# A mask table read by SyncE, zero products between TensorE's own, and loads behind flags in an attention and MLP kernel

## The chip, the cores and the metric

The kernel runs on one core of one Trainium2 chip. A time is the device time of one execution in microseconds (us). The time before is 322.92 us, the median of 9 executions (320.95 to 325.45). One more execution was recorded by the hardware profiler; its span, from the first to the last instruction, is 321.2 us and its own time 322.98 us. All shares and waits below come from that one.

## The reference

Two blocks follow each other. The first is block-sparse attention over 4 batches, 8 heads, 768 positions and 64 values per head:

```python
scores = scale * np.matmul(q, k.transpose(0, 1, 3, 2))
# mask: neighbouring blocks of 32, the first and last block, 3 sampled blocks for each block row
scores = np.where(mask, scores, -1000000000.0)
attn = softmax(scores)
x = np.matmul(attn, v)
```

The mask is the same for all batches and heads. The second block mixes tokens and channels, with `w_tok` 768x768, `w_ch1` 512x2048 and `w_ch2` 2048x512:

```python
u = x + lam * einsum('ts,bsd->btd', w_tok, alpha1 * x + beta1)
out = u + lam * (np.maximum((alpha2 * u + beta2) @ w_ch1, 0) @ w_ch2)
```

Inputs and the output are float32; the kernel computes its products in 16-bit types.

## The kernel before

**Units and pairs.** The 32 (batch, head) combinations are worked off as 16 pairs of heads, pair `p` being two heads of batch `p // 4`. Each pair has nine units (`NU`), and a unit is 128x1024 scores in one PSUM tile `sps`, of which there are two. TensorE makes the scores, ScalarE turns them into exponentials in an `eT` tile, TensorE multiplies these by V (with a column of ones, so that the row sums come out too) into the PSUM tile `ops`, and VectorE divides (L614, L617) into `x_sb`.

**Two ways of masking.** The first six pairs (`single`, L642, L657, L682) carry the mask in the scores product itself, as 24 more rows of the contraction. The other ten (`paired`, L720, L746, L751, L778) make the scores of two heads side by side in the two halves of the array and clamp the exponentials against a table `maskT`, 128 x 9 x 512 in f16: VectorE takes the minimum at L751. The table's 24 distinct rows are made by `mrow` (L470); `mout` (L476) writes them to DRAM, each 32 times, and `min_` (L479) reads the whole table back. Both transfers are issued by POOL.

**Heads.** Q and K reach SBUF by POOL's loads (L305, with a cast to bf16, in `ld` buffers), VectorE casts them into a `rel` buffer (L492; two buffers), and they are transposed into `qx` and `kx`: for the first six pairs by TensorE (L211) with copies out of PSUM by ScalarE (L269) or VectorE (L271), for the others by two DMA transposes that SyncE issues (L581). V is copied into a `vext` buffer (L800).

**The MLP.** When a pair is normalised, VectorE makes `a1p`, TensorE multiplies it by the transposed `w_tok` (L854), VectorE adds (L864) and makes `ub` (L870), which is transposed into `uT` by TensorE (batch 0) or by a DMA (L901). When a batch's `uT` is complete, its first layer (L927), the ReLU (L938 on ScalarE, L942 on VectorE) and the second layer (L972, in the PSUM tiles `cp` and, once attention is over, `ops`) can run. `w2b`, which holds the second layer's weights, is scaled by `lam` on VectorE (L455) after it has landed.

**The order.** While the kernel is built, a planner decides the order in which each engine's instructions are written. Every piece of work is a `Job` with an engine, an assumed duration, a priority and the buffers that it takes and gives back. The planner goes through time, and whenever an engine is free it takes the ready job of the best priority. The chip then runs each engine's instructions in that order. POOL's loads have a fixed order, and the planner has its own notion of when a load lands (`xfer`, `dma_free`). A `gate` holds scores back that run too far ahead of the MLP. PV of batch 0 may use `ops` or `cp` (the `take` at the PV job), since the MLP does not need `cp` yet. At the start, `keep_warm` issues products of a zero tile `warm` (L169), which shares its buffer with the `eT` tiles.

Of the kernel before, what the change touches and what calls it, by code (L numbers as in the profile page):

```python
# [12 lines left out]
F16 = mybir.dt.float16  # L13
BF = mybir.dt.bfloat16
# [6 lines left out]
S = 768  # L21
D = 64
BLK = 32
NBLK = S // BLK
# [3 lines left out]
P = 128  # L28
NT = S // P
# [6 lines left out]
NU = 9  # L36
NS = NPAIR * NU
NPE = 6
NET = 11
LEAD = 18  # L40
NLD = 7
AHEAD = 13000.0
SCALE = 1.0 / 8.0
EXPB = -0.35667494
# [21 lines left out]
def kernel(  # L66
# [19 lines left out]
    nc = tc.nc  # L86
# [22 lines left out]
    wk = ctx.enter_context(tc.tile_pool(name="work", bufs=1))  # L109
# [50 lines left out]
    for i in range(1, NQB):  # L160
        nc.sync.dma_start(kx[i][MB, :], ind_dr.ap())

    warm = wk.tile([P, 512], BF, name="warm", tag="eT", bufs=NET)
    nc.vector.memset(warm[:], 0.0)
    wps = ps.tile([P, 512], FP, name="cp", tag="cp", bufs=1)

    def keep_warm(n, w):
        for _ in range(n):
            nc.tensor.matmul(wps[:, 0:w], warm[:, 0:P], warm[:, 0:w], start=True, stop=True)  # L169

    keep_warm(9, 512)
    for t in vext:
# [21 lines left out]
            op1=ALU.mult,  # L194
        )

    rel0 = wk.tile([P, 2, NT, 2 * D], BF, name="rel", tag="rel", bufs=2)

    def first_cast(a):
        for i, src in enumerate((q2f, k2f)):  # L200
# [31 lines left out]
    for j in range(2, NQB):  # L232
# [11 lines left out]
    DRAIN = 166.0  # L244
    free_at = dict(NONE=0.0, PE=T0, ACT=T0, DVE=T0, POOL=4800.0, SP=T0)
    slots = dict(
        sps=2, mm=2, cp=1, ops=1, eT=NET, head=NQB, vext=NV, ld=NLD, rel=2,
        x=NXB, uT=3, hts=2, a1p=2, ub=2, ot=2, w2b=1,
    )
    jobs = []  # L250
# [2 lines left out]
    class Job:  # L253
        def __init__(self, eng, dur, prio, fn, deps=(), take=(), give=(), lat=None):
            self.eng = eng if isinstance(eng, tuple) else (eng,)
            self.dur, self.prio, self.fn = dur, prio, fn
            self.deps = list(deps)
            self.take, self.give = take, give
            self.lat = lat
            self.alt = {}  # L260
            self.xfer = None
            self.done = None
            self.gate = None
            self.n = len(jobs)
            jobs.append(self)
# [31 lines left out]
    def Load(xfer, prio, fn, deps=(), take=()):  # L297
        j = Job("POOL", 720.0, prio, fn, deps, take)
        j.xfer = xfer
        return j  # L300

    def load(name, src_ap, shape, dt, tag, bufs, xfer, prio, deps=(), take=()):
        def fn():
            t = wk.tile(shape, dt, name=name, tag=tag, bufs=bufs)
            nc.gpsimd.dma_start(t[:], src_ap)  # L305
            return t

        return Load(xfer, prio, fn, deps, take)
# [3 lines left out]
    w2tile = []  # L312
    wtk_tile = []

    def load_pair(p, prio, which="qkv"):
        for src, dt, nm in ((q, BF, "q2"), (k, BF, "k2"), (v, F16, "v2")):
            if p == 0 and nm != "v2" or nm[0] not in which:
                continue
            ld[p, nm] = load(
                nm, pair_ap(src, *pairs[p]), [P, 2, NT * D], dt, "ld", NLD,  # L320
                1300.0 if p < 2 else 980.0, prio, take=("ld",),
            )

    def plain(eng, dur, prio, fn, deps=(), **kw):
        return Job(eng, dur, prio, fn, deps, **kw)
# [57 lines left out]
        load_w1(g, next(order))  # L383
    load_pair(5, next(order))
    load_pair(6, next(order))
    mout_prio = next(order)
    w2_prio = [next(order) for _ in range(2)]
    min_prio = next(order)
    w2_prio += [next(order) for _ in range(2)]
    for p in range(7, len(pairs)):  # L390
        load_pair(p, next(order))

# [71 lines left out]


    rows = maskT[:].rearrange("p u c -> p (u c)")[:, 0:S]
    mask_dr = nc.dram_tensor("mask_rows", [NBLK, BLK, S], F16, kind="Internal").ap()

    def mrow():
        nc.vector.tensor_scalar(  # L470
# [2 lines left out]
        )  # L473

    def mout():
        nc.gpsimd.dma_start(mask_dr, rows[MB, :].unsqueeze(1).broadcast_to([NBLK, BLK, S]))  # L476

    def min_():
        nc.gpsimd.dma_start(  # L479
            maskT[:].rearrange("p u c -> p (u c)"),  # L480
            mask_dr.rearrange("g r c -> (g r) c").rearrange("(p o) c -> p (o c)", o=NT),
        )

    j = Job("DVE", 400.0, (3, 3, 9), mrow, [wtok_jobs[-1]])
    j = Load(5000.0, mout_prio, mout, [j])
    mask_jobs = [Load(5000.0, min_prio, min_, [j])]

# [9 lines left out]
        return ld[p, nm].out[:]  # L499

    head_ready = {}
    after = []

    def slot_of(p):
        return (2 * NPE + p - NPE) % NQB
# [2 lines left out]
    for p in range(len(pairs)):  # L508
# [25 lines left out]
        elif p < NPE:  # L534

            def rel_of(p, i):
                def f():
                    if i == 0:
                        rels[p] = wk.tile([P, 2, NT, 2 * D], BF, name="rel", tag="rel", bufs=2)
                    return rels[p][:, :, :, i * D : (i + 1) * D]  # L540

                return f

            cq = cast_job(p, 0, "q2", rel_of(p, 0), (2, p, 0), ("rel",))
            ck = cast_job(p, 1, "k2", rel_of(p, 1), (2, p, 1), (), [cq])
            prev = head_ready[2 * p - 1]
            for a in range(2):
                h = 2 * p + a

                def tr(p=p, a=a, h=h):  # L550
                    tl["hd", h] = transposes(rels[p], a)

                def cpq(eng, h=h):
                    copy(eng, qx[h % NQB][0:D, :], tl["hd", h][0:D, :])

                def cpk(eng, h=h):
                    copy(eng, kx[h % NQB][0:D, :], tl["hd", h][D:P, :])

                jt = Job("PE", mmt(NT, P), (2, p, a), tr, [ck, prev], take=("mm", "head"),
                         give=("rel",) if a else ())  # L560
                j1 = Copy((1, p, a), cpq, [jt])
                j2 = Copy((1, p, a), cpk, [jt])
                prev = head_ready[h] = Job("NONE", 0.0, (0,), lambda: None, [j1, j2], give=("mm",), lat=0.0)
        else:

            def stage_of(p, i):
                def f():
                    if i == 0:
                        rels[p] = wk.tile([P, 2, NT, P], BF, name="rel", tag="rel", bufs=2)
                    return rels[p][:, i, :, :].rearrange("p o (h d) -> p h o d", h=2)  # L570

                return f

            cq = cast_job(p, 0, "q2", stage_of(p, 0), (3, p, 0), ("rel",))
            if p > NPE + 1:
                after.append((cq, (p - 3) * NU))
            ck = cast_job(p, 1, "k2", stage_of(p, 1), (3, p, 1), (), [cq])

            def xt(p=p):
                for i, dst in enumerate((qx, kx)):  # L580
                    nc.sync.dma_start_transpose(  # L581
                        dst[slot_of(p)][:].rearrange("p (o c) -> p o c", o=NT),
                        rels[p][:, i, :, :].rearrange("p o c -> p (o c)"),
                    )

            prev = [head_ready[2 * NPE - 1]] if p == NPE else [head_ready[2 * p - 2]]
            jx = Job("SP", 2600.0, (1, p), xt, [ck] + prev, take=("head",), lat=2500.0,
                     give=("rel",))
            jx.slow = True
            head_ready[2 * p] = head_ready[2 * p + 1] = jx  # L590
# [36 lines left out]
    def single(p):  # L627
# [3 lines left out]
        for u in range(NU):  # L631
# [40 lines left out]
            for si, (s0, s1) in enumerate(segs):  # L672
# [20 lines left out]
                give = ("eT",) if s1 == hi else ()  # L693
                if s1 == 2 * HT:
                    give += ("vext",)
                take = ((("ops", "cp") if b == 0 else ("ops",), ("opsel", p, a)),) if first else ()
                prev_pv = Job("PE", mmt(s1 - s0, D + 1), (2, i, si), pv, deps, take=take, give=give)
                last_pv = prev_pv
                if s1 % HT == 0:
# [110 lines left out]
            single(p)  # L810
    for j, i in after:
        j.deps.append(qk_jobs[i])

# [237 lines left out]
    heapq.heapify(events)  # L1053
    seq = 100
    early = set()
    loads = sorted((j for j in jobs if j.xfer is not None), key=lambda j: (j.prio, j.n))
    t = 0.0
    left = len(jobs)
    pe_idle = []
    while left:  # L1060
        moved = True
        while moved:
            moved = False
            for e in free_at:
# [19 lines left out]
                for tk in j.take:  # L1084
# [6 lines left out]
                            st["ch2"] = True  # L1091
                    else:
                        slots[tk] -= 1
                j.out = j.fn(e) if len(j.eng) > 1 else j.fn()
                if getattr(j, "ch", False):
                    st["ch"] += j.dur
                if e == "PE" and t - free_at[e] > 1:
                    pe_idle.append((free_at[e], t))
                dur = j.alt.get(e, j.dur)
# [2 lines left out]
                free_at[e] = t + dur  # L1102
                lat = j.lat if j.lat is not None else DRAIN + SEM if e == "PE" else SEM
                j.done = t + dur + lat
                if j.xfer is not None:
                    dma_free[0] = max(dma_free[0], t + 2300.0) + j.xfer
                    j.done = dma_free[0] + 200.0
                    loads.pop(0)
                seq += 1
                heapq.heappush(events, (j.done, seq, j))  # L1110
                if e == "PE":
# [16 lines left out]
        while events and events[0][0] <= t:  # L1128
            _, _, j = heapq.heappop(events)
            if j is None:  # L1130
                continue
            for g in j.give:
                if isinstance(g, tuple):
                    slots[tl.pop(("slot", g))] += 1
                else:
                    slots[g] += 1
            for s in succ.get(j.n, ()):
                if (j.n, s.n) in early:
                    continue
                waiting[s.n] -= 1  # L1140
                if not waiting[s.n]:
                    for e in s.eng:
                        by_eng[e].append((t, s))
# [31 lines left out]
```

The softmax here doesn't subtract the row's maximum and nothing guards it: scores larger than these inputs give would overflow.

## Time and profile before

| | |
|---|---|
| median of 9 executions | 322.92 us |
| profiled execution, its own time | 322.98 us |
| its span | 321.2 us |
| granted TensorE clock over the span | 0.995 |
| TensorE (PE) busy | 307.0 us, 96%, 3238 products |
| ScalarE (ACT) busy | 208.0 us, 65% |
| VectorE (DVE) busy | 207.4 us, 65% |
| POOL busy | 44.3 us, 14% |
| DMA | 31.95 MB, mean 99 GB/s |
| mask write, issue to landing | 12.6 us |
| mask read, issue to landing | 9.0 us |

PE is TensorE's products and PEld its weight loads, which overlap them; POOL is GpSimd and SP is SyncE, which only issues transfers here. Products are pipelined and their ends are modelled, so a product's recorded duration is a latency: what counts is the pitch from one to the next. A line such as `X <- Y: 3.5, 8, 0.8` in the waits says that X's engine stood for Y's result for 3.5 us in total, 8 times, at most 0.8 us. A name such as L927 is a line of the kernel file.

### The profile page before, as it was taken

To read this page: it belongs to the slowest core of one execution; us is meant where nothing else is said; L and a number is where in the kernel's file an instruction comes from. 1 tells how busy PE (TensorE), PEld (TensorE's weight loads), DVE (VectorE), ACT (ScalarE), POOL (GpSimd) and SP (SyncE) were. 2 spreads that over 40 slices of the span, in tenths; PEclk is the share of its full clock that TensorE was granted. 3 is DMA by queue.
4 is the path that set the end of the run, shared out by engine and by line. 5 is a ranking of instruction groups with operands and counts; after the bars stand their busy time and mean duration, and the time that the engine had idled before them with its cause. 6 is when DMAs were issued, how large, how long until landed. Compare 5 with 4: busy or idle time off the path is not lost.

```text
span 321.2 us, 7610 instructions
## 1 busy us (share of the span) xinstructions
PE 307.0 (96%) x3238; PEld 189.1 (59%) x3238; DVE 207.4 (65%) x406; ACT 208.0 (65%) x264; POOL 44.3 (14%) x69
## 2 busy tenths in 40 slices
PE   7889989899699999999999999999999999999996
PEld 3566868667444556565655556565655575555544
DVE  4558977779578887877977688868677660201001
ACT  4979899897656667756686567755784526354530
POOL 4638142515001010100100000000000000000000
PEclk9979999999999999999999999999999999999999
DMA  6999999999999397724581231311100201201102
GB/s 147 182 246 203 210 236 173 265 191 124 138 130 208 63 123 80 101 59 111 56 111 46 57 61 24 59 25 69 23 4 35 76 16 24 100 0 53 48 23 75
DMA packets 46774, 31.95 MB, mean 99 GB/s; under 512 B 27516, under 2 KB 42264, under 8 KB 46612
## 3 DMA queue, kind: packets, MB, share of 16 engines
q0 software_dynamic: 16496, 17.83, 35.1%
q1 hardware_dynamic: 29992, 13.40, 22.1%
q8 instruction: 25, 0.41, 0.5%
q10 hardware_dynamic: 252, 0.24, 0.3%
q14 instruction: 9, 0.07, 0.1%
HBM read 32.04 MB, written 7.47 MB: 123 GB/s over the span
## 4 chain that ended last, share of the span: by engine, by line
PE 77%; DMA 13%; ACT 4%; DVE 2%; POOL 2%; issue 1%; DVEq 0%; ACTq 0%
PE mm L927 22%; PE cp L972 22%; PE mm L854 8%; PE ops L778 8%; PE sps L720 7%; DMA w2b<-in_moe_w_ch_dram 5%; DMA kx<-rel 4%; PE ops L972 4%; ACT eT L657 3%; DMA wtk<-in_moe_w_tok_dram 3%; PE sps L642 2%; PE sps L927 2%; PE ops L682 1%; DMA q2f<-in_q_dram 1%; DVE hts L942 1%
## 5 line engine op out<-in xcount | busy, mean ns | idle before, releaser
L746 ACT ACTIVATE eT<-sps 128x1024 f16<-128x1024 f32 x90 | 88.3, 1020 | 31.8 <-PE sps L720 30.5
L927 PE MATMUL mm<-uT,w1b 128*128 128x384 bf16 x472 | 90.6, 326 | 2.9 <-DVE x_sb L864 2.5
L938 ACT ACTIVATE hts<-mm,b1t 128x384 bf16<-128x384 f32 x91 | 52.9, 581 | 57.7 <-PE mm L927 55.0
L972 PE MATMUL cp<-w2b,hts 128*128 128x512 bf16 (+1 forms) x336 | 80.4, 374 | 0.3 <-DVE hts L942 0.3
L751 DVE TENSOR_TENSOR eT<-eT,maskT 128x1024 f16<-128x1024 f16 x90 | 61.0, 686 | 13.5 <-ACT eT L746 13.4
L927 PEld LDWEIGHTS <-w1b 128*128 128x128 bf16 x512 | 46.9, 97 | 37.0 <-issue 7.4
L972 PEld LDWEIGHTS <-hts 128*128 128x128 bf16 x400 | 36.5, 98 | 34.7 <-issue 1.4
L657 ACT ACTIVATE eT<-sps 128x1024 f16<-128x1024 f32 (+1 forms) x55 | 52.7, 1015 | 4.8 <-PE sps L642 4.3
L989 DVE TENSOR_TENSOR ot<-x_sb,cp 128x512 f32<-128x512 f32 (+1 forms) x21 | 14.1, 673 | 46.3 <-PE cp L972 45.7
L778 PEld LDWEIGHTS <-eT 128*128 128x128 f16 x720 | 29.7, 97 | 16.4 <-issue 3.6
L854 PE MATMUL mm<-a1p,wtokT 128*128 128x128 bf16 x576 | 36.6, 219 | 0.1
L642 PE MATMUL sps<-qx,kx 88*128 88x512 bf16 (+1 forms) x144 | 31.9, 330 | 4.4 <-ACT eT L657 3.5
L778 PE MATMUL ops<-vext,eT 128*128 128x65 f16 x720 | 35.5, 194 | 0.0
L854 PEld LDWEIGHTS <-wtokT 128*128 128x128 bf16 x576 | 33.0, 98 | 1.9 <-issue 0.5
L720 PE MATMUL sps<-qx,kx 64*128 64x512 bf16 (+1 forms) x240 | 27.3, 327 | 0.0
L942 DVE TENSOR_SCALAR hts<-mm,b1t 128x384 bf16<-128x384 f32 x27 | 16.5, 616 | 9.9 <-PE mm L927 9.7
L682 PEld LDWEIGHTS <-eT 128*128 128x128 f16 x432 | 19.4, 98 | 6.0 <-issue 0.8
L864 DVE TENSOR_TENSOR x_sb<-x_sb,mm 128x384 f32<-128x384 f32 x32 | 17.6, 551 | 7.3 <-PE mm L854 7.2
L642 PEld LDWEIGHTS <-kx 88*128 88x128 bf16 x144 | 12.8, 99 | 10.2 <-issue 5.6
L870 DVE TENSOR_TENSOR ub<-x_sb,a_bc 128x384 bf16<-128x384 f32 x32 | 17.2, 554 | 0.3
L720 PEld LDWEIGHTS <-kx 64*128 64x128 bf16 x240 | 8.1, 94 | 15.2 <-issue 12.5
L617 DVE TENSOR_TENSOR x_sb<-ops,rcp 128x384 f32<-128x384 f32 x28 | 15.6, 558 | 1.0
(74 smaller groups left out, 222.6 us busy)
## 6 DMA issues: line engine op xcount, KB each, us to landing
out_dram<-ot SPq DMA_DIRECT2D x23, 256.0 KB, 2.0
v<-in_v_dram POOLq DMA_DIRECT2D x16, 192.0 KB, 6.5
q<-in_q_dram POOLq DMA_DIRECT2D x15, 192.0 KB, 10.5
k<-in_k_dram POOLq DMA_DIRECT2D x15, 192.0 KB, 6.9
w1b<-in_moe_w_ch_dram POOLq DMA_DIRECT2D x4, 512.0 KB, 10.4
w2b<-in_moe_w_ch_dram POOLq DMA_DIRECT2D x4, 512.0 KB, 14.9
wtk<-in_moe_w_tok_dram POOLq DMA_DIRECT2D x3, 384.0 KB, 10.1
mask_rows<-maskT POOLq DMA_DIRECT2D x1, 1152.0 KB, 12.6
```

Of the source, the lines that this page charges most:

```text
L642: nc.tensor.matmul(sps[:, f - u * UN : f - u * UN + w], kx[h][0:KC, ts(jt, P)], qx[h][0:KC, c : c + w], start=True, stop=True,)
L657: nc.scalar.activation(eT[:, c], sps[:, c], AF.Exp, bias=EXPB, scale=SCALE)
L682: nc.tensor.matmul(ops[p, a][:, t * VW : t * VW + D + 1], eTs[p, u][:, ts(i - u * GU, P)], vx[:, a, jt, 0 : D + 1], start=(i % HT == 0), s ...
L720: nc.tensor.matmul(sps[:, a * 512 + lo : a * 512 + lo + w], kx[sl][r, ts(jt, P)], qx[sl][r, c : c + w], start=True, stop=True,)
L746: nc.scalar.activation(eT[:], sps[:], AF.Exp, bias=EXPB, scale=SCALE)
L751: nc.vector.tensor_tensor(out=e, in0=e, in1=maskT[:, u, :].unsqueeze(1).broadcast_to([P, 2, 512]), op=ALU.min,)
L778: nc.tensor.matmul(ops[p, a][:, t * VW : t * VW + D + 1], eTs[p, u][:, a * 512 + c * P : a * 512 + (c + 1) * P], vx[:, a, jt, 0 : D + 1], ...
L854: nc.tensor.matmul(tp[:, j, :], wtokT[:, s, ts(3 * g + j, P)], tl["a1p", p][:, s, :], start=(s == 0), stop=(s == NT - 1),)
L927: nc.tensor.matmul(hp[:, 0:HS], w1b[:, dk, ts(f, P)], uTs[b][:, dk, ts(hf, HS)], start=(dk == 0), stop=(dk == 3),)
L938: nc.scalar.activation(hts[kk][:, f, :], hp[:, 0:HS], AF.Relu, bias=b1t[:, f : f + 1], scale=1.0)
L942: nc.vector.tensor_scalar(out=hts[kk][:, f, :], in0=hp[:, 0:HS], scalar1=b1t[:, f : f + 1], scalar2=0.0, op0=ALU.add, op1=ALU.max,)
L972: nc.tensor.matmul(cps[kk, mi][:, 0:w], hts[kk][:, nk, ts(m, P)], w2tile[0][:, nk, lo : lo + w], start=(nk == 0), stop=(nk == 15),)
```

## The change

The change has five parts.

1. **The mask table.** Only the 24 rows are written to DRAM, once, by SyncE. SyncE reads the table with 18 transfers: transfer `c` fills the partitions `c`, `c + 16`, and so on, eight in all, and repeats one DRAM row over up to six of a partition's table rows; where the six straddle a block border, it is split in two. All this hangs in the planner's order on the scores of unit 28 (`MASK_AT`), no longer on the last of the `w_tok` copies. The four `w2b` loads come one after another in POOL's order. The planner knows the read as a job of SyncE that also delays loads in flight (`bulk`).
2. **Zero products.** `fill` writes products of the zero tile in front of a TensorE job wherever the planner sees TensorE idle for longer, as wide as the idle time allows (up to 512 columns), until the first second-layer job. They go to `cp`, so PV of batch 0 uses `ops` alone. The zero tile has a buffer of its own.
3. **Flags.** From pair 8 on, each load of q, k and v is preceded on POOL by a copy of one element of `flag` into `held_`, and VectorE sets that element (`raise_flag`). The planner ties the flag of pair `p` to the scores of unit `9 * (p - 2) + 2`, and 3 and 6 more for k and v; it used to tie the cast of q to unit `9 * (p - 3)`.
4. **Three stages.** `rel` has three buffers instead of two.
5. `ld` has six buffers instead of seven.

The line numbers shift: L642 becomes L676, L657 L691, L682 L716, L720 L754, L746 L780, L751 L785, L778 L812, L492 L529, L581 L615, L854 L889, L927 L962, L972 L1007.

```diff
-NLD = 7
+NLD = 6
+HOLD = 2
+MASK_AT = 28
...
-    warm = wk.tile([P, 512], BF, name="warm", tag="eT", bufs=NET)
+    warm = pp.tile([P, 512], BF, name="warm", tag="warm")
...
+    def fill(ns):
+        while ns > 60.0:
+            w = min(512, int(ns * 2.4))
+            keep_warm(1, w)
+            ns -= w / 2.4 + 3.0
...
-    rel0 = wk.tile([P, 2, NT, 2 * D], BF, name="rel", tag="rel", bufs=2)
+    rel0 = wk.tile([P, 2, NT, 2 * D], BF, name="rel", tag="rel", bufs=3)
...
+            if held is not None:
+                nc.gpsimd.tensor_copy(out=held_[0:1, held : held + 1], in_=flag[0:1, held : held + 1])
             t = wk.tile(shape, dt, name=name, tag=tag, bufs=bufs)
             nc.gpsimd.dma_start(t[:], src_ap)
...
+    def raise_flag(p, i):
+        c = 3 * p + i
+
+        def fn():
+            nc.vector.memset(flag[0:1, c : c + 1], 0.0)
+
+        j = Job("DVE", 70.0, (0, p), fn)
+        after.append((j, (p - 2) * NU + HOLD + 3 * i))
+        return [j]
...
-    mask_dr = nc.dram_tensor("mask_rows", [NBLK, BLK, S], F16, kind="Internal").ap()
+    mask_dr = nc.dram_tensor("mask_rows", [NBLK, S], F16, kind="Internal").ap()
...
     def mout():
-        nc.gpsimd.dma_start(mask_dr, rows[MB, :].unsqueeze(1).broadcast_to([NBLK, BLK, S]))
+        nc.sync.dma_start(mask_dr, rows[MB, :])
...
     def min_():
-        nc.gpsimd.dma_start(
-            maskT[:].rearrange("p u c -> p (u c)"),
-            mask_dr.rearrange("g r c -> (g r) c").rearrange("(p o) c -> p (o c)", o=NT),
-        )
...
+        dst = maskT[:].rearrange("p u c -> p (u c)").rearrange("p (o w) -> p o w", o=NT)
+        src = mask_dr.rearrange("(m f) w -> m f w", f=3)
+        for c in range(16):
+            o = 0
+            while o < NT:
+                f, r = divmod(NT * c + o, BLK)
+                e = min(NT, o + BLK - r)
+                nc.sync.dma_start(
+                    dst[c:P:16, o:e, :], src[:, f, :].unsqueeze(1).broadcast_to([8, e - o, S])
+                )
+                o = e
+
+    mrow_job = j = Job("DVE", 400.0, (2, 3, 9), mrow)
+    j = Job("SP", 400.0, (0, 0), mout, [j], lat=2500.0)
+    j = Job("SP", 7200.0, (0, 1), min_, [j])
+    j.bulk = 5500.0
+    mask_jobs = [j]
...
-                take = ((("ops", "cp") if b == 0 else ("ops",), ("opsel", p, a)),) if first else ()
+                take = ((("ops",), ("opsel", p, a)),) if first else ()
...
+                if e == "PE" and not st["ch2"]:
+                    fill(t - free_at[e] - 60.0)
```

## The prediction

> **What bounds the kernel now.** I read the slices of the page first, then a table of stretches, the waits of each engine, the timeline around the largest hole, and the chain in order of time for the pitch of each product.
>
> ```profile
> PE   7889989899699999999999999999999999999996
> ACT  4979899897656667756686567755784526354530
> PEclk9979999999999999999999999999999999999999
> ```
>
> TensorE leaves room only in the first third of the span, and there ScalarE is as full; one slice has a low clock. The stretches (busy us of PE, PEld, DVE, ACT, POOL, then clock, DMA share, GB/s):
>
> ```profile
> 18.00:20.00 2.00, 1.83 (x16) 1.28 (x17) 0.56 (x1) 1.74 (x2) 0.73 (x1) 0.58 1.08 205
> 20.00:22.00 2.00, 2.00 (x22) 1.76 (x20) 1.01 (x3) 1.08 (x2) 0.99 (x2) 0.56 1.20 319
> 60.00:77.00 17.00, 16.40 (x236) 12.05 (x234) 14.19 (x29) 14.14 (x15) 4.70 (x7) 1.00 1.30 187
> 77.00:100.00 23.00, 19.89 (x182) 10.96 (x182) 16.65 (x34) 14.84 (x20) 4.43 (x7) 1.00 1.41 140
> 100.00:260.00 160.00, 159.84 (x1726) 93.45 (x1725) 125.63 (x231) 103.64 (x131) 6.99 (x10) 1.00 0.38 66
> 260.00:318.00 58.00, 58.00 (x351) 32.63 (x349) 8.54 (x14) 23.61 (x41) 0.00 (x0) 1.00 0.13 43
> ```
>
> From 100 us on TensorE never rests, so nothing but its own work counts there. The waits of TensorE and VectorE (total us, times, longest):
>
> ```profile
> PE sps L642 <- ACT eT L657: 3.5, 8, 0.8
> PE mm L927 <- DVE x_sb L864: 2.5, 1, 2.5
> PEld L778 <- DVE eT L751: 3.1, 10, 0.4
> DVE rel L492 <- DMA kx<-rel: 5.0, 2, 3.7
> ```
>
> The second and the fourth are one event, which the timeline shows:
>
> ```profile
> 79.64 3.84 SPq L581 DMA_TRANSPOSE qx<-rel  x1
> 83.53 4.73 SPq L581 DMA_TRANSPOSE kx<-rel  x1
> 86.80 0.36 DVE L492 COPY rel<-q 128x768 bf16<-128x768 bf16 x1 [3.68 <-DMA kx<-rel]
> 88.28 0.81 PE L927 MATMUL mm<-uT,w1b 128*128 128x384 bf16 x4 [2.46 <-DVE x_sb L864]
> ```
>
> The cast of pair 9 finds both `rel` buffers in use: pair 8's two transposes, which elsewhere issue in 1.2 to 1.6 us each (medians), take 8.6 us while the DMA share is 1.41. VectorE stands, the additions behind the cast are late, TensorE stands 2.5 us.
>
> TensorE's pitch, from the chain in order of time:
>
> ```profile
> 65.92 0.65 PE mm L927 x4
> 100.82 1.09 PE ops L778 x36
> 101.91 0.86 PE cp L972 x4
> 38.42 0.87 PE sps L642 x5
> ```
>
> These are 0.163, 0.030 and 0.216 us per product, and 0.435 per single unit of scores (two units in 0.87). With 0.056 for a 128-wide product (18 in 1.00) and 0.22 for a paired unit, instruction counts times pitch give 287.8 us of TensorE work, 61.5 before the first paired scores product (at 77.0 us, unit 54) and 226.2 behind it. Call the two parts stage one and stage two. The last product ends at 318.0; the span is 321.2, the profiled execution 323.0, the median 322.9.
>
> Stage two: 241.0 = 226.2 of work + 11.2 + 3.6. The 11.2 are 45 switches between full-array products and the half-height paired ones at 0.25 us each (mean gap around them after 100 us, where no wait is recorded). The 3.6 lie before 100 us, 3.1 of them named waits. Stage one: 77.0 = 61.5 of work + 3.9 of start + 11.6 idle, of which 1.7 is half clock. ScalarE sets its length: 54 exponentials at 0.95 to 1.0, 13 PSUM copies at 0.80, one ReLU at 0.58, and 5.0 idle.
>
> [...] 0.58 and 0.56 at 18 to 22 us, behind a sparse stretch (1.17 us busy between 16 and 18). [...]
>
> **The change part by part.**
>
> *Order of work.* Counted in the instruction lists of the two builds. Before unit 54 TensorE does 8 first-layer products instead of 16 and no second-layer ones instead of 4: 1.3 + 0.9 = 2.2 us move to stage two. With one zero product there (0.2), stage two has 228.6: **+2.4**. ScalarE loses three copies (3 x 0.80) and gains a ReLU (0.58): **-1.8** on stage one. VectorE takes the copies (3 x 0.55), hidden in its idle time: it is busy 14.2 of 17 us before unit 54; without that cover they would cost 1.65.
>
> *Zero products.* 31 new ones, 5.65 us in all, 5.4 in stage one. The planner puts each where it expects TensorE to wait. Bounds: zero if the wait is there, +5.4 if none is. TensorE's 9.9 us of full-clock idle in stage one exceeds them, and the spots follow waits for ScalarE, which the waits show. They should lift the sparse 15 to 20 us and keep the clock: gain 0 to 1.7; I take 1.3, since part of that hole is the arrival of `wtk` (0.9), which stays.
>
> *PV of batch 0 has one PSUM slot.* A head's first PV now waits for reciprocal and multiply (0.19 + 0.56 and two semaphores, about 1.1). The new order has 1.2 to 2.2 us of TensorE work (partly zeros) between heads. Cost 0 to 12 x 0.2. For misfit of zeros and slot together I take **+0.5**.
>
> *Mask.* The POOL write of 1152 KB (12.6 us to landing) shrinks to 36 KB; the read is 18 SyncE issues after one write, at unit 28 or so (42 us). At 0.4 us an issue (the store's 0.37) that is 7.2 us, moving 5 to 12 with traffic, so over by about 60. SyncE's next work, pair 6's transposes, needs unit 40's heads (59.9 us before); they are needed at unit 54. That is five us of cover if they land as slowly as before (9.6), ten at the 3.7 of later ones; beyond it each us is lost in full. The first use of the mask is at 79. With half the mask's bytes gone and POOL not waiting 10.6 us for the write, all four `w2b` loads and pair 7 issue some 9 us earlier.
>
> *Three stages, held loads.* The third `rel` buffer lets pair 9's cast pass; pairs 8 on are loaded one by one from unit 56, so the DMA engines are freer when pair 8 is transposed. Of the 3.6 us I leave 0.5: **-3.1** (bounds -3.6 and 0). Each held load adds a VectorE memset (0.07, a vext memset took 0.078) and a POOL copy (0.26, from `hold`). From flag to cast VectorE has 3.9 to 13.8 us of own work by these durations; a load issued after 97 us landed in 3.4 to 6.4, mean 4.4. So a few casts will stand on their load, and min, ReLU and additions behind them too; TensorE's weight loads already wait on L751 (3.1 us). Bounds 0 and 7; I take **+0.7**. One `ld` buffer less moves early loads by one cast; they were issued 12 us ahead: 0.
>
> *Sum.* Stage one -1.8 - 1.3 + 0.5 = -2.6, so unit 54 at 74.4. Stage two +2.4 - 3.1 + 0.7 = 0.0. Span 321.2 - 2.6 = 318.6; with the 1.8 around it 320.4, against 323.0 profiled and 322.9 median: -0.8%.
>
> **Rivals.**
>
> *The zeros are not free.* For: TensorE work in stage one rises to 64.8 of some 70 us[...]. Against: ScalarE, which sets the waits, is slower than or equal to what it was. All of it: stage one takes 64.8 + 3.9 + 9.9 = 78.6 instead of 74.4, so 324.6. Half of it: 322.5.
>
> *Held loads come late (slower).* The loads of before lay ready long ahead; now the slack is about 1 us. If landing is 6.4 (the slowest seen late) plus 0.3, against 4 to 6 us of VectorE work, a mean of 0.3 us on each of 24 loads reaches TensorE: 7.2 instead of 0.7, so 326.9. It decides from a mean of 0.2 us per load (4.8; 324.5). Against: VectorE has 34 us of idle between 100 and 260.
>
> *All reliefs in full.* Clock 1.7, no misfit, no late load, waits gone: -3.5 in stage one, 2.4 - 3.6 in stage two: span 316.5, 318.3.
>
> *The relief changes nothing that counts.* The transposes are slow anyway because the `w2b` and pair 7 loads still crowd them, and the clock dips elsewhere: -3.1 and -1.3 go, +1.8: 324.8.
>
> **Numbers.** Chances: forecast 0.45, all reliefs 0.15, half-cost zeros 0.18, late loads 0.14, no relief 0.08. Within 0.5% is about what a measurement of this kernel tells from no change, 321.3 to 324.5. The forecast's own range is 318.8 to 322.0; a sixth of it lies over 321.3, and so does most of the zeros' case. Faster 0.58, same 0.24, slower 0.18. The range leaves out late loads at full price and the edge of the best case: 317.0 to 325.0.
>
> **What would show it.** Unit 54's first scores product near 74.4 and no half clock between 15 and 25 us; few waits on `sps` beside the zero products; no wait of VectorE on the `kx` transposes, no 2.5 us wait at L962; casts at L529 after 80 us waiting under 1 us. I am wrong if the casts stand on `in_q_dram` for several us in total, if the first transposes come behind the mask reads after 65 us, or if unit 54 comes at 76 or later.

## The result, and the profile after

The changed kernel takes 319.9 us (median of 18 executions, 318.7 to 320.8), against 322.75 for the kernel before beside it (55 executions, 319.7 to 325.5): a ratio of 0.992, with a 95% interval of 0.990 to 0.994. The prediction was 320.4. The ratios, here and below, leave out executions more than 1.5% above the fastest of the same kernel. The profiled execution took 318.9 us, with a span of 317.1, against 323.0 and 321.2 before.

First the slices of the page, as they were shown for the kernel before: busy tenths of TensorE and ScalarE in 40 slices, and the granted clock.

```profile
PE   7999999999999999999999999999999999999995
ACT  4989889997775666656765667647775526253620
PEclk9999999999999999999999999999999999999999
```

But for the first slice, the slices of seven and eight tenths that TensorE had in the first third are gone, and so is the slice of low clock. The table of stretches for the same windows (busy us of PE, PEld, DVE, ACT, POOL, then clock, DMA share, GB/s; the share adds up the packets' times over 16 engines, and so can pass 1: 1.10 and 1.13 in the first two rows):

```profile
18.00:20.00 2.00, 1.73 (x27) 1.29 (x26) 1.20 (x4) 1.95 (x3) 0.73 (x1) 1.00 1.10 201
20.00:22.00 2.00, 1.52 (x22) 1.07 (x20) 1.10 (x3) 2.00 (x4) 1.13 (x2) 1.00 1.13 348
60.00:77.00 17.00, 16.96 (x238) 12.29 (x237) 15.15 (x32) 15.44 (x18) 0.00 (x0) 1.00 0.68 120
77.00:100.00 23.00, 22.94 (x234) 12.90 (x233) 18.76 (x39) 15.81 (x21) 4.25 (x9) 1.00 0.46 73
100.00:260.00 160.00, 159.53 (x1704) 93.35 (x1701) 124.40 (x249) 99.64 (x127) 20.64 (x40) 1.00 0.45 77
```

Two columns matter. From 77 to 100 us TensorE is busy 22.94 of 23 us, where it was 19.89: that is the relief. And the DMA share of that window is 0.46 instead of 1.41, because the held loads no longer crowd into it: POOL issues 4 loads from 66 to 100 us where it issued 11, and in the runs below the share is 0.50 with the flags alone and 1.50 with the third buffer alone. POOL's 20.64 us after 100 are the copies of flags and the held loads' issue. The waits (total us, times, longest):

```profile
PE sps L676 <- ACT eT L691: 0.8, 2, 0.6
PEld L812 <- DVE eT L785: 3.4, 10, 0.4
DVE rel L529 <- DMA k<-in_k_dram: 3.0, 2, 2.2
POOL held L315 <- DVE flag L335: 136.7, 24, 29.8
```

TensorE's 2.5 us on an addition and VectorE's 5.0 us on the `kx` transposes are no longer in the list. New are POOL's 136.7 us for flags, which is what the flags are for. VectorE's 3.0 us for `k` are mostly not the flags' doing: 2.2 of them fall at 12.9 us, on an early load, as 1.7 did at 12.1 us before; only 0.8, at 214 us, are for a held load. Last the timeline of SyncE's queue (start, us, line, transfer):

```profile
43.63 0.30 SPq L502 DMA_DIRECT2D mask_rows<-maskT  x1
47.65 15.89 SPq L514 DMA_DIRECT2D maskT<-mask_rows  x18
63.71 1.39 SPq L615 DMA_TRANSPOSE qx<-rel  x1
65.21 1.22 SPq L615 DMA_TRANSPOSE kx<-rel  x1
...
85.65 1.21 SPq L615 DMA_TRANSPOSE qx<-rel  x1
88.67 1.21 SPq L615 DMA_TRANSPOSE kx<-rel  x1
```

The 18 mask reads take 15.9 us, not the 5 to 12 of the prediction; the first DMA transposes of `qx` and `kx` start behind them at 63.7, and pair 8's two (85.65 and 88.67) now issue in 1.2 us each, where they took 3.84 and 4.73.

By position: the first paired scores product (unit 54) starts at 73.09 us instead of 77.01; the last TensorE product ends at 313.63 instead of 318.05; stage two lasts 240.54 instead of 241.04.

### The profile page after: what moved, and what is told of

Its sections match the earlier page's. It is cut to its first block, busy times and chain, and to the rows that moved or that the text cites. A ratio compares the mean times of both kernels' runs of the same rounds, so it can differ in the third digit from the quotient of the medians.

```text
span 317.1 us, 7729 instructions
## 1 busy us (share of the span) xinstructions
PE 309.5 (98%) x3269; PEld 189.4 (60%) x3269; DVE 209.0 (66%) x432; ACT 204.5 (64%) x262; POOL 50.8 (16%) x91
## 4 chain that ended last, share of the span: by engine, by line
PE 85%; ACT 6%; DMA 3%; DVE 2%; POOL 1%; issue 1%; ACTq 0%
PE mm L962 23%; PE cp L1007 22%; PE mm L889 10%; PE ops L812 8%; PE sps L754 7%; PE sps L676 4%; PE ops L1007 4%; ACT eT L691 4%; PE ops L716 2%; DMA k<-in_k_dram 2%; PE sps L962 2%; DVE hts L977 1%; DMA q2f<-in_q_dram 1%; ACT kx L279 1%; ACT qx L279 1%
## 5 line engine op out<-in xcount | busy, mean ns | idle before, releaser
L780 ACT ACTIVATE eT<-sps 128x1024 f16<-128x1024 f32 x90 | 88.2, 1020 | 29.4 <-PE sps L754 28.5
L962 PE MATMUL mm<-uT,w1b 128*128 128x384 bf16 x472 | 90.6, 326 | 0.5
L1007 PE MATMUL cp<-w2b,hts 128*128 128x512 bf16 (+1 forms) x336 | 79.9, 374 | 0.0
L785 DVE TENSOR_TENSOR eT<-eT,maskT 128x1024 f16<-128x1024 f16 x90 | 60.6, 686 | 13.2 <-ACT eT L780 12.7
L962 PEld LDWEIGHTS <-w1b 128*128 128x128 bf16 x512 | 47.2, 98 | 35.4 <-issue 5.1
L1007 PEld LDWEIGHTS <-hts 128*128 128x128 bf16 x400 | 36.6, 98 | 33.3 <-issue 0.3
L691 ACT ACTIVATE eT<-sps 128x1024 f16<-128x1024 f32 (+1 forms) x55 | 52.3, 1017 | 3.7 <-PE sps L676 3.4
L812 PEld LDWEIGHTS <-eT 128*128 128x128 f16 x720 | 29.0, 97 | 16.5 <-issue 5.9
L889 PE MATMUL mm<-a1p,wtokT 128*128 128x128 bf16 x576 | 36.8, 219 | 0.0
L812 PE MATMUL ops<-vext,eT 128*128 128x65 f16 x720 | 35.2, 194 | 0.0
L889 PEld LDWEIGHTS <-wtokT 128*128 128x128 bf16 x576 | 33.3, 98 | 2.2
L676 PE MATMUL sps<-qx,kx 88*128 88x512 bf16 (+1 forms) x144 | 31.5, 325 | 1.5 <-ACT eT L691 0.8
L315 POOL COPY held<-flag 1x1 bf16<-1x1 bf16 x24 | 8.3, 347 | 136.7 <-DVE flag L335 136.7
L754 PE MATMUL sps<-qx,kx 64*128 64x512 bf16 (+1 forms) x240 | 27.3, 327 | 0.0
L716 PEld LDWEIGHTS <-eT 128*128 128x128 f16 x432 | 19.0, 97 | 5.8 <-DVE x_sb L651 0.8
L716 PE MATMUL ops<-vext,eT 128*128 128x65 f16 x432 | 21.0, 193 | 0.0
L651 DVE TENSOR_TENSOR x_sb<-ops,rcp 128x384 f32<-128x384 f32 x32 | 17.8, 558 | 1.1
```

Source lines behind the costliest of these rows:

```text
L676: nc.tensor.matmul(sps[:, f - u * UN : f - u * UN + w], kx[h][0:KC, ts(jt, P)], qx[h][0:KC, c : c + w], start=True, stop=True,)
L691: nc.scalar.activation(eT[:, c], sps[:, c], AF.Exp, bias=EXPB, scale=SCALE)
L716: nc.tensor.matmul(ops[p, a][:, t * VW : t * VW + D + 1], eTs[p, u][:, ts(i - u * GU, P)], vx[:, a, jt, 0 : D + 1], start=(i % HT == 0), s ...
L754: nc.tensor.matmul(sps[:, a * 512 + lo : a * 512 + lo + w], kx[sl][r, ts(jt, P)], qx[sl][r, c : c + w], start=True, stop=True,)
L780: nc.scalar.activation(eT[:], sps[:], AF.Exp, bias=EXPB, scale=SCALE)
L785: nc.vector.tensor_tensor(out=e, in0=e, in1=maskT[:, u, :].unsqueeze(1).broadcast_to([P, 2, 512]), op=ALU.min,)
```

## The experiments

All ratios are to the kernel before, run beside (medians 322.86, 323.24 and 323.09 in three sets); an interval of about ±0.3% means that differences between two variants under some 1 us are not told apart.

**The third `rel` buffer, from both sides.** First the kernel before with three buffers and nothing else. The order of instructions on every engine is that of before.

```diff
-    rel0 = wk.tile([P, 2, NT, 2 * D], BF, name="rel", tag="rel", bufs=2)
+    rel0 = wk.tile([P, 2, NT, 2 * D], BF, name="rel", tag="rel", bufs=3)
...
-        sps=2, mm=2, cp=1, ops=1, eT=NET, head=NQB, vext=NV, ld=NLD, rel=2,
+        sps=2, mm=2, cp=1, ops=1, eT=NET, head=NQB, vext=NV, ld=NLD, rel=3,
```

> The kernel before with three rel buffers instead of two; the order on every engine is the same. If the buffer alone ends the wait: the 3.7 us of VectorE and the 2.5 us of TensorE go and the time is 319.3 to 320.3 against 322.8. Rival (the slow transposes hold up something else, the cast of pair 10 for one): 322 to 323.

Measured: 319.7 us, ratio 0.992 (0.990 to 0.995). One buffer alone makes the whole gain of the change. (Its profiled execution, 318.2 us, is the fastest of its 15.) In its timeline of SyncE's queue pair 8's transposes are as slow as before, and the stretch around them shows TensorE standing no longer, under the same DMA share:

```profile
78.86 5.15 SPq L581 DMA_TRANSPOSE qx<-rel  x1
84.06 3.78 SPq L581 DMA_TRANSPOSE kx<-rel  x1
```

```profile
77.00:100.00 23.00, 22.98 (x234) 13.06 (x232) 20.11 (x39) 17.34 (x23) 3.99 (x7) 1.00 1.50 142
```

So the buffer does not make the transposes faster; VectorE no longer stands behind them. Then the reverse: the changed kernel with two `rel` buffers, again with the same order on every engine as the changed one.

```diff
-    rel0 = wk.tile([P, 2, NT, 2 * D], BF, name="rel", tag="rel", bufs=3)
+    rel0 = wk.tile([P, 2, NT, 2 * D], BF, name="rel", tag="rel", bufs=2)
...
-        sps=2, mm=2, cp=1, ops=1, eT=NET, head=NQB, vext=NV, ld=NLD, rel=3,
+        sps=2, mm=2, cp=1, ops=1, eT=NET, head=NQB, vext=NV, ld=NLD, rel=2,
```

> The changed kernel with two rel buffers instead of three; the order on every engine is the same. Theory (the third buffer ended the wait of pair 9's cast): a wait of VectorE on a transpose near 80 to 100 us comes back and the time is 322 to 323. Rival (the loads behind flags come so late that pair 7's transposes have long read their buffer): no such wait, 319.9 as with three.

Measured: 319.2 us, ratio 0.990 (0.987 to 0.993), no slower than the change. In the changed kernel the third buffer, to which the prediction gave most of its -3.1, does nothing: something else has cured the same wait.

**Flags alone and flags with the buffer.** The kernel before with the flags, six `ld` buffers and the loads' planner term, but two `rel` buffers and the old mask route:

```diff
-NLD = 7
+NLD = 6
+HOLD = 2
...
+        after.append((j, (p - 2) * NU + HOLD + 3 * i))
...
+                nc.gpsimd.tensor_copy(out=held_[0:1, held : held + 1], in_=flag[0:1, held : held + 1])
...
-            if p > NPE + 1:
-                after.append((cq, (p - 3) * NU))
```

> The kernel before with the flags and six ld buffers alone: two rel buffers, old mask route, two PSUM slots, no zeros; TensorE's work ahead of unit 54 stays 61.5 us. Theory (holding the loads from pair 8 on back ends the wait of pair 9's cast as the third buffer does, since that cast comes later and the transposes are quick): 319.3 to 320.5. Rival (flags only protect the new mask route): 322 to 323.5.

Measured: 320.4 us, ratio 0.995 (0.993 to 0.997). TensorE's gaps of more than 0.1 us in stage two fall from 3.1 us to 0.2. Its profiled execution is the slowest of 22 (322.9 us), so what it shows of the old mask route is one case and not the rule. The timeline of VectorE:

```profile
58.44 1.29 DVE L476 TENSOR_TENSOR w2b<-w2b,lam_bcb 128x1024 bf16<-128x1024 bf16 x2 [1.77 <-DMA w2b<-in_moe_w_ch_dram]
61.59 0.69 DVE L476 TENSOR_TENSOR w2b<-w2b,lam_bcb 128x1024 bf16<-128x1024 bf16 x1 [1.86 <-DMA w2b<-in_moe_w_ch_dram]
```

and the stretch in which TensorE stands behind that:

```profile
60.00:70.00 10.00, 7.68 (x92) 5.14 (x89) 5.00 (x10) 5.46 (x7) 0.00 (x0) 0.83 1.20 199
```

VectorE stands for `w2b`, which landed late, and TensorE's next transposes stand 2.3 us for VectorE. In this execution two of the `w2b` loads are issued behind a POOL wait of 10.9 us for the mask write.

Both cures together, the edit of flags alone and beside it three buffers:

```diff
-    rel0 = wk.tile([P, 2, NT, 2 * D], BF, name="rel", tag="rel", bufs=2)
+    rel0 = wk.tile([P, 2, NT, 2 * D], BF, name="rel", tag="rel", bufs=3)
...
+            hold_ = p > NPE + 1
```

> The kernel before with the flags, six ld buffers and three rel buffers. Theory (flags and third buffer are two cures of one wait, so they do not add): 319.3 to 320.2, as with the third buffer alone (319.7). Rival (they add): 316.5 to 318.

Measured: 320.5 us, ratio 0.995 (0.993 to 0.997). The order on every engine is that of flags alone. The cures do not add: with either one the wait is gone, and a second one has nothing left to cure. The six `ld` buffers were never tried alone, so what they do by themselves is not shown.

**The change without its flags.** Loads of q, k and v are free to run ahead, and the cast of q is tied to unit `9 * (p - 3)` as before.

```diff
-            hold_ = p > NPE + 1
+            hold_ = False
...
+            if p > NPE + 1:
+                after.append((cq, (p - 3) * NU))
```

> The changed kernel without flags: loads from pair 8 on go as soon as a buffer is free, and the cast of q is tied to unit 9 (p - 3) as before; six ld buffers, zeros, new mask route and three rel buffers stay. Theory (flags are free, and with three rel buffers also of no use): 319.3 to 320.3. Rival A (they cost VectorE and POOL time or late casts): 318 to 319. Rival B (without them transfers crowd the transposes again): 321 to 322.

Measured: 325.6 us, ratio 1.008 (1.005 to 1.011): slower than the kernel before. The waits, then SyncE's timeline, then one piece of the chain in order of time:

```profile
PE sps L756 <- DMA kx<-rel: 5.4, 1, 5.4
```

```profile
47.91 16.43 SPq L514 DMA_DIRECT2D maskT<-mask_rows  x18
64.71 1.31 SPq L617 DMA_TRANSPOSE qx<-rel  x1
66.14 2.06 SPq L617 DMA_TRANSPOSE kx<-rel  x1
68.31 3.73 SPq L617 DMA_TRANSPOSE qx<-rel  x1
72.14 4.47 SPq L617 DMA_TRANSPOSE kx<-rel  x1
```

```profile
66.14 13.19 DMA kx<-rel
```

The mask reads take 16.4 us here too, and the first transposes start only 1.0 us later than in the change. What differs comes after: pair 6's `kx` needs 13.2 us from issue to the product that uses it, and TensorE stands 5.4 us in front of unit 54 (79.37 us instead of 73.09). The stretch from 70 to 80 us, here and then in the changed kernel, shows what the transposes meet:

```profile
70.00:80.00 10.00, 3.74 (x59) 2.74 (x59) 4.77 (x11) 2.63 (x3) 2.14 (x3) 0.92 1.43 131
```

```profile
70.00:80.00 10.00, 9.96 (x121) 6.55 (x122) 8.74 (x17) 7.72 (x10) 0.89 (x2) 1.00 0.24 49
```

The DMA share is 1.43 against 0.24: in the kernel without flags eight loads of pairs 8 to 10 are issued between 49 and 73 us. The hole has a price of its own, in the table of stretches behind it:

```profile
78.00:80.00 2.00, 0.63 (x6) 0.28 (x6) 0.00 (x0) 0.00 (x0) 0.00 (x0) 0.62 1.54 127
```

With it, from 78.5 us, the clock is halved for 6.83 us. TensorE's order is that of the changed kernel until well behind unit 54, but for five zero products fewer, so the hole is not one of order. How much of it the free loads make and how much the earlier casts that this edit also allows is not separated. The flags, with the later casts that follow them, are thus what makes the new mask route bearable.

**The mask route.** The changed kernel with the POOL route of before (the planner's order follows it: 16 instead of 8 first-layer products stand before unit 54):

```diff
-        nc.sync.dma_start(mask_dr, rows[MB, :])
+        nc.gpsimd.dma_start(mask_dr, rows[MB, :].unsqueeze(1).broadcast_to([NBLK, BLK, S]))
...
-    j = Job("SP", 400.0, (0, 0), mout, [j], lat=2500.0)
-    j = Job("SP", 7200.0, (0, 1), min_, [j])
+    j = Load(5000.0, mout_prio, mout, [j])
+    mask_jobs = [Load(5000.0, min_prio, min_, [j])]
```

> The changed kernel with the mask route of before: POOL writes each row 32 times and reads the table once, between the w2b loads; zeros, flags and three buffers stay, the planner's order follows (16 first-layer products ahead of unit 54 instead of 8, zeros 0.7 us more). Theory (the mask's traffic and POOL's wait make w2b, pair 7 and the transposes late): 321 to 323. Rival (mask traffic was covered all along): 319.5 to 320.3.

Measured: 321.0 us, ratio 0.996 (0.994 to 0.999). With flags the new route, with the order that follows from it, is thus about 1.0 us better than the old (319.9 against 321.0; the intervals of the two ratios meet, at 0.9936 and 0.9938). Most of this goes with the clock: 12 of the 22 executions with the old route have a mean clock of 0.998 or more and take 320.3 us, the other ten 323.8, while all of the change's have 0.998 or more (319.8). What makes the old route lose its clock more often is not shown.

To see the route without flags I put zeros and then the mask into the kernel before with three buffers. Zeros first, kept to the time in which `cp` is free, so that PV of batch 0 keeps both slots:

```diff
-    rel0 = wk.tile([P, 2, NT, 2 * D], BF, name="rel", tag="rel", bufs=2)
+    rel0 = wk.tile([P, 2, NT, 2 * D], BF, name="rel", tag="rel", bufs=3)
...
+                if e == "PE" and not st["ch2"] and slots["cp"] > 0:
+                    fill(t - free_at[e] - 60.0)
```

> The kernel before with three rel buffers and zero products, but both PSUM slots kept: zeros only where the planner sees cp free (4.7 us of them). Set against the third buffer alone (319.7). Theory (zeros stand in waits and buy the half clock's 1.7 us in the executions that have it): clock 1.0 in every execution and 318.2 to 319.2. Rival (they cost as much as they buy): 319.4 to 320.5.

Measured: 319.7 us, ratio 0.990 (0.987 to 0.994), against 319.7 with three buffers alone. Six of seven executions have the full clock over the whole span, against 4 of 15 without the zeros; the time is the same. Here the zeros cost about what they buy: at full clock the executions take 318.8 us without them (4) and 319.6 with them (6). Then the same kernel with the new mask route besides (the planner's order follows: 12 first-layer products before unit 54 instead of 16):

```diff
-        nc.gpsimd.dma_start(mask_dr, rows[MB, :].unsqueeze(1).broadcast_to([NBLK, BLK, S]))
+        nc.sync.dma_start(mask_dr, rows[MB, :])
...
+    j = Job("SP", 400.0, (0, 0), mout, [j], lat=2500.0)
+    j = Job("SP", 7200.0, (0, 1), min_, [j])
+    j.bulk = 5500.0
```

> As the kernel before with three rel buffers and zeros in a free cp, with the 18 mask reads of SyncE in addition; two PSUM slots, no flags, seven ld buffers. If the mask route is worth the 1.0 us by which the changed kernel with the old route was slower: 317.2 to 318.5. Rival (that 1.0 us came from the order and the 0.7 us more of zeros there): the same as without the new mask route, 318.2 to 319.2.

Measured: 322.9 us, ratio 1.001 (0.999 to 1.004). The new route, with its order, costs 3.2 us without flags (322.9 against 319.7). Part of it is lost clock: with a mean clock of 0.998 or more the difference is 2.3 (321.9 in 10 executions against 319.6 in 6). The profiled execution is the longest of 22 (328.0 us) and so no more than a hint; it has the wait of the kernel without flags: TensorE stands 4.4 us for `kx` in front of unit 54. The change without flags is another 2.7 us slower than this kernel (325.6); they differ in the `ld` buffers, the PSUM slot and the zeros, and which of them does it is open.

**Zeros and the PSUM slot.** The changed kernel without its 31 new zero products, which are no part of the output; the order of everything else is unchanged:

```diff
-                if e == "PE" and not st["ch2"]:
-                    fill(t - free_at[e] - 60.0)
```

> The changed kernel without its 31 zero products (5.65 us of TensorE work); every other instruction and the order on every engine stay. Theory (the zeros stand in waits and keep the clock): the half clock comes back once between 15 and 25 us and the time is 320.0 to 321.2, against 319.9 with them. Rival (the zeros take real TensorE time, since the changed kernel shows no wait of TensorE between 25 and 40 us): the time falls to 317 to 319.

Measured: 321.1 us, ratio 0.995 (0.993 to 0.997): the zeros bring 1.2 us. They bring it elsewhere than I had said. The stretches, first without zeros, then in the changed kernel:

```profile
18.00:20.00 2.00, 1.69 (x26) 1.24 (x25) 1.38 (x4) 1.95 (x3) 0.73 (x1) 1.00 1.11 206
...
42.00:44.00 2.00, 0.87 (x13) 0.54 (x12) 1.87 (x6) 1.30 (x2) 1.64 (x3) 1.00 1.31 204
44.00:46.00 2.00, 1.43 (x17) 1.04 (x17) 2.00 (x5) 1.78 (x3) 2.00 (x3) 0.66 1.30 188
46.00:48.00 2.00, 2.00 (x45) 1.60 (x42) 1.54 (x5) 1.30 (x2) 1.52 (x4) 0.50 1.20 195
```

```profile
42.00:44.00 2.00, 2.00 (x19) 1.16 (x20) 1.87 (x6) 1.19 (x2) 1.53 (x3) 1.00 1.31 204
```

Without zeros TensorE is busy 0.87 of 2 us from 42 to 44, and from 44.6 the clock is halved for 6.83 us; with them it is busy throughout and the clock stays. At 18 us, where the kernel before lost its clock, this execution keeps it without any zero. Executions without zeros at a mean clock of 0.988 or 0.989 take 321.2 us (10 of them), those at 0.995 take 319.8 (3), which is the time of the change; all executions of the change have 0.998 or more. The half clock of 6.83 us in this profiled execution goes with a mean of 0.989, the one of 3.41 us in that of the kernel before with 0.995. By these means the zeros remove the executions with a long half clock, not a fixed 1.7 us.

The same without zeros, but with both slots for PV of batch 0:

```diff
-                if e == "PE" and not st["ch2"]:
-                    fill(t - free_at[e] - 60.0)
...
-                take = ((("ops",), ("opsel", p, a)),) if first else ()
+                take = ((("ops", "cp") if b == 0 else ("ops",), ("opsel", p, a)),) if first else ()
```

> The changed kernel without zeros and with both PSUM slots for PV of batch 0; flags, new mask route, three rel buffers and six ld buffers stay. Set against the changed kernel without zeros (321.1). Theory (the single slot costs 0.4 to 1 where no zeros fill its waits): 320.1 to 320.8, with half clock in some executions. Rival (the slot costs nothing): 320.9 to 321.4.

Measured: 321.0 us, ratio 0.995 (0.993 to 0.997), against 321.1 with the one slot. With this order 11 of 22 executions have a mean clock of 0.998 or more without any zero, and take 320.5. And the change with both slots and zeros only where `cp` is free:

```diff
-                take = ((("ops",), ("opsel", p, a)),) if first else ()
+                take = ((("ops", "cp") if b == 0 else ("ops",), ("opsel", p, a)),) if first else ()
...
-                if e == "PE" and not st["ch2"]:
+                if e == "PE" and not st["ch2"] and slots["cp"] > 0:
```

> The changed kernel with both PSUM slots, and zeros only where cp is free (4.5 us of them). Theory (the slot's cost goes, the clock stays full): 318.6 to 319.5, better than the changed kernel. Rival (the zeros filled the waits of the single slot, so nothing is left to gain): 319.6 to 320.5.

Measured: 320.6 us, ratio 0.994 (0.992 to 0.996). With a second slot ScalarE has 13 PSUM copies before unit 54 again, where the change has 10, and in the profiled execution unit 54 comes at 76.23 instead of 73.09, at full clock. With a mean clock of 0.998 or more 21 and 19 executions stand at 320.4 and 319.8. So the one slot costs nothing here; if anything the order that the planner writes with it is the better one. Beside the zeros the order is that of the run before: in it the zeros bring 0.4 us (321.0 to 320.6), which the intervals do not tell from nothing.

Last the slot in the kernel before with three buffers:

```diff
-    rel0 = wk.tile([P, 2, NT, 2 * D], BF, name="rel", tag="rel", bufs=2)
+    rel0 = wk.tile([P, 2, NT, 2 * D], BF, name="rel", tag="rel", bufs=3)
...
-                take = ((("ops", "cp") if b == 0 else ("ops",), ("opsel", p, a)),) if first else ()
+                take = ((("ops",), ("opsel", p, a)),) if first else ()
```

> The kernel before with three rel buffers, and PV of batch 0 in ops alone; no zeros, old mask route, no flags. Set against the third buffer alone (319.7). Theory (the single PSUM slot costs, since a head's PV now waits for the division): 320.2 to 321.4. Rival (TensorE always has 1.1 us of other work between heads): 319.4 to 320.0.

Measured: 320.1 us, ratio 0.990 (0.986 to 0.994), against 319.7: 0.4 at most, not told apart from none.

## Why the prediction was right, and where its steps were not

The total was right within 0.5 us, and the wait that it was built on is the one that went. The sum itself, made for the profiled execution, gave a span of 318.6 where 317.1 was measured: stage one 1.3 shorter than said, stage two 0.5 shorter, the end behind the last product 0.3 longer. That the median came closer is because the profiled execution (318.9) is a us below it. So the closeness of the total is in part luck: several of the terms below were off and made up for each other, or did not show.

*Three stages, held loads: -3.1.* The size is right: stage two has 11.9 us beside its work instead of 14.8, so 2.9 less, and TensorE's gaps over 0.1 us there fall from 3.1 to 0.2. The attribution failed: "the third `rel` buffer lets pair 9's cast pass" names one of two cures, each enough alone (319.7 with the buffer, 320.4 with the flags) and not additive (320.5 with both). In the changed kernel it is the flags that act: pair 8's transposes are quick (1.21 us each to issue), and two buffers do as well as three (319.2 and 319.9).

*Late casts: +0.7.* The mechanism did not occur. The held loads landed in 3.3 to 6.2 us, as assumed, and VectorE stands for one of them once, 0.8 us at 214 us, where TensorE shows no gap; so the rival of late loads fell too. Yet the flags are not free. In the kernel before, stage two lasts 238.11 us with flags, with two `rel` buffers and with three, and 237.36 with three buffers and no flags (237.35 with zeros beside them), all without a half clock in it. These 0.75 us have the size of the term, by luck: with flags alone no cast waits for a held load. The planner writes another order with flags, and in it TensorE's short pauses between first-layer products add up to some 2.1 us instead of 1.2; why is not shown.

*Mask: over by about 60.* This is the step that failed, though it did not show in the total. 18 reads took 15.9 us instead of 5 to 12. The sum had taken 0.4 us an issue; each takes 0.57 at least, the starts are 0.6 apart at best, which is 11 us for 18, and the rest is pauses of the queue (4.5 us in seven waits for earlier reads). The 5 of the range was my estimate for the transfer alone, which no trace showed; the measured 15.9, at a DMA share of 1.11 from 48 to 63 us, is three times that. The cover of ten us for landing was real and just sufficed: the first transposes start at 63.7, unit 54 at 73.1 without a wait. By the run without flags, it held only because the flags kept the other loads out of the way. I had listed the mask's cost and the flags' benefit as separate sums. They are one: the route costs 3.2 us without flags (322.9 against 319.7), and the change without flags is 5.7 us slower than the change. The rival that ended on the slower side should have been this one; mine put it at the casts.

*Order of work: +2.4 and -1.8.* Stage two's TensorE work is 228.61 instead of 226.23, +2.38. ScalarE's copies before unit 54 fall from 13 to 10, 2.4 us; the added ReLU does not show before unit 54 (one before, one after), so -2.4 instead of -1.8. The two-slot variant, with 13 copies, has unit 54 3.1 us later, which points the same way.

*Clock: -1.3, in stage one.* The half clock (3.41 us from 18.3 us, hence the clock of 0.58 and 0.56 in the two stretches from 18 to 22) is gone, as said. But the place was wrong: unit 24 starts at 36.75 instead of 36.33, with one more exponential behind it (25 instead of 24), so at most some 0.6 us was gained up to there. Stage one as a whole was shorter by 3.9 instead of 2.6, and that lies between units 24 and 54 (40.7 to 36.3), where three copies (2.4), one exponential that moved ahead (1.0) and VectorE's wait for `w2b` (1.7 before, no longer listed) are gone. How these overlap I did not separate. The size was near: in the profiled execution of the kernel before with three buffers, which has its order of work and no half clock, unit 54 comes at 75.89 instead of 77.01, 1.1 us earlier, and a wait of 0.9 us for `wtk` is gone in it too. What the zeros do for the time in the changed kernel is shown by the runs: 1.2 us, and in the profiled execution without them there is a half clock of 6.83 us at 44 us. In the two other orders in which they were tried they bring 0.4 us and nothing.

*Zeros and slot: +0.5 of misfit.* No run isolates it in the changed kernel; with the order of before the zeros cost some 0.8 us at full clock (318.8 against 319.6, few executions). The waits of TensorE on `sps` fall from 3.5 to 0.8 us, so most zeros took the place of waiting.

*A term counted twice.* The 11.2 us for switches between full-array and paired products held the 2.5 us wait in front of one of them; the gaps around paired products without it come to 9.0 us, 0.20 each, before and after. The 3.6 of waits beside it were therefore partly counted again; since both kernels share the switches, the difference was not touched. The reading "after 100 us, where no wait is recorded" was thus wrong. Some 2.7 us of stage two, in both kernels, then belong to none of the terms.

What stays open: flags alone and both cures stand 0.7 to 0.8 us behind the third buffer alone, which is no more than the intervals of the medians allow, though the profiled executions show the same 0.75 us in stage two; what it consists of is open. No version that ran is clearly better than the change. Its five parts together give what one buffer gives (319.9 against 319.7).

## What to carry to other kernels

When two parts of a change stand on the same wait, price the wait once and ask of each part what it does alone: here a third buffer and a hold on the loads each removed the same wait, worth some 3 us. A long burst on a queue is priced with the traffic that its successors then meet: eighteen mask reads in front of the transposes cost nothing that shows where the DMA engines were quiet behind them (a share of 0.24 from 70 to 80 us), and without the hold on the loads, at shares of 1.41 and 1.43, the kernels that have them were 3.2 and 5.7 us slower. Zero products can be worth having where a sparse stretch loses the clock, as 0.87 us of work in 2 did here; they brought 1.2 us in one order of work and nothing clear in two others. They should be judged over many executions: of the changed kernel's 14 without zeros, 10 had a mean clock of 0.988 or 0.989, three 0.995 and one 0.998.

## What the runs showed of the hardware

- Half clocks of two lengths occur in the profiled executions: 3.41 us in the kernel before (from 18.33 us), 6.83 us in the changed kernel without zeros (from 44.6 us) and without flags (from 78.5 us, 4.5 us into a hole of 5.4 us in TensorE's work). In the first two a sparse stretch lies ahead: 1.17 us of work in 2 (16 to 18 us) and 0.87 in 2 (42 to 44 us). How little work it takes is not shown: the kernel before with three buffers had 1.24 us in 2 (20 to 22 us) and a clock of 1.00 over its whole span.
- The time does not go with the mean clock alone. The kernel before with three buffers took 318.8 us at full clock (4 executions) and 320.9 at 0.995 (10), the kernel before beside it 322.5 (4) and 322.8 (25). Where the half clock lay in executions without a profile is not recorded.
- A DMA transpose that SyncE issues in 1.2 us at a DMA share of 0.46 (the changed kernel, pair 8) took 3.7 to 5.2 us to issue at shares of 1.41 to 1.50 (the kernel before, with two and with three buffers, and the change without flags).
- Eighteen reads of 24 to 72 KB, into eight partitions each, took 15.9 and 16.4 us on SyncE's queue in traffic (0.57 us each at least, and pauses), where one read of 1152 KB in all, issued by POOL, had landed 9.0 us after its issue.
